# The second MoE's first product by Strassen's algorithm, its weight sums kept in DRAM

## Chip, cores and metric

The kernel runs on one core of a Trainium2 chip. The metric is the time of one execution on the device in microseconds, the median of several runs. A core has TensorE (PE, matmuls), VectorE (DVE), ScalarE (ACT), GpSimd (POOL) and the queues that issue DMAs, of which SyncE's (SP) is used most here.

## What is computed

Attention with rotary embedding, then two feed-forward layers. Only the last one is touched by the change:

```python
# q, k, v: (4, 8, 576, 64)
attn = softmax(rot(q) @ rot(k).T / 8) @ v
x = attn as (2304, 512)                       # 4 * 576 tokens, 8 * 64 features
# first MoE: w1, w2, w3 (512, 768), w_out (768, 512)
y = maximum(maximum(x @ w1, x @ w2), x @ w3) @ w_out
# second MoE: w_in (512, 2048), w_out (2048, 512)
h = y @ w_in
g = h / (1 + exp(-h))
out = g @ w_out                               # (2304, 512) float32
```

## The kernel before

The kernel works at more than float16 precision: each operand of a product is scaled by a power of two and split into a float16 high and low part (`split`, two instructions: the high part on ScalarE, the low part on VectorE), and a product is three float16 matmuls, high-high, high-low and low-high. A matmul here has a 128 x 128 stationary operand and a moving one of 256 or 320 columns.

The instructions are written in program order in a framework that places them on the engines with a planner of its own: an instruction that is ready by the planner's reckoning goes ahead of an earlier one that isn't, and each engine then runs its own list in the order fixed at build time. Buffers are rings with a fixed number of slots (`Ring`), and an instruction that takes a slot waits until the slot's last user is done. A PSUM bank is waited for as a whole.

Attention runs first, the first MoE (`moe1`) beside it, batch by batch, and its last batch alone. It computes `y` and stores it in the DRAM scratch `yscr`. Its groups go to five PSUM banks (rings `ps_m` and `ps_g`), and ScalarE (L548) and VectorE (L550, L557) evacuate them. In the attention part `narrow_w2` has turned the second MoE's weights into float32 and stored them in the DRAM scratches `zscr["wi"]` and `zscr["wo"]`.

Beside the last batch of `moe1` the weights of the second MoE are made ready. `load_w2` reads `w_in` back and splits its 16 pieces of 512 columns in place (`WI`, L154 and L159). `prep_wo7` makes the seven sums of four quarter blocks of `w_out` that Strassen's algorithm wants, in 8 tiles `w7[f]`: two loads, four differences of 256 columns (L758, on VectorE or GpSimd), two splits (L763, L764). Four of the tiles are made here, the other four beside the start of `moe2`.

`moe2` works in 9 blocks `jb` of 256 tokens, in four units `u` each. `s1(jb, u)` computes 4 of the 16 blocks of 128 features of `h`, each with 4 x 3 matmuls (L796), 48 in all, into two PSUM banks of one ring, and the next unit takes the other ring (`ps_m`, tag "m", and `ps_b`, tag "mb", two banks each). ScalarE applies Silu from PSUM (L797), GpSimd makes four sums (L803), ScalarE and VectorE split the seven forms in pieces of 768 and 1024 columns (L808, L809) into `g7`. `s2(jb, u)` computes the unit's share of the second product by Strassen's algorithm (Winograd's form): 7 products x 2 x 3 = 42 matmuls (L827), accumulated over the units in four banks `a`, `b`, `c`, `d`. `close(jb)` combines these (L836 to L846) and stores the block. In program order `s1` runs two units ahead of `s2`. `y_load` and `y_split` prepare `y` for 512 tokens at a time (largest magnitude over a block with L146 and `all_max`, which takes a slot of `ps_m`; four splits).

## Time and profile before

| | us |
|---|---|
| median of three runs | 1049.77 (1049.08 to 1051.04) |
| the profiled execution | 1053.66 |
| its span, first to last instruction | 1051.9 |
| TensorE busy in it | 983.7 |
| VectorE, ScalarE, GpSimd busy | 596.2, 585.1, 397.1 |
| mean granted TensorE clock | 0.972 |

The page gives the busy time of each engine over the whole span. A table of windows gives it for a chosen stretch, with the granted TensorE clock as a share of 2.4 GHz. The timeline lists instructions in order of time: start, duration, engine, line, tile written and tiles read, and in brackets how long the engine was idle before it and what released it. Groups of instructions give the mean duration of one form of one line.

### The profile page before, as it was taken

The page shows a single profiled execution, that of the slowest core. Times are in us where ns is not written, and L with a number is a line of the kernel's source. Part 1 is how long each engine was busy: PE and PEld are TensorE (multiplying, and loading weights), DVE is VectorE, ACT ScalarE, POOL GpSimd, SP SyncE. Part 2 cuts the span into 40 slices and gives each one's busy share as a digit, 9 for nine tenths or more (in the row PEclk, how much of TensorE's full clock was granted, in tenths as well). Part 3 has the DMA queues.
Part 4 walks back from the last instruction along what each step waited for, and adds up shares of the span by engine and source line. Part 5 has one row for each costly group of instructions (what it writes and reads, how often), then busy time and mean ns, then how long its engine had stood idle before and what let it go on. Part 6 is the DMA issues. An engine that isn't in the chain of part 4 may idle for free.

```text
span 1051.9 us, 18993 instructions
## 1 busy us (share of the span) xinstructions
PE 983.7 (94%) x7426; PEld 739.4 (70%) x7426; DVE 596.2 (57%) x1090; ACT 585.1 (56%) x1287; POOL 397.1 (38%) x420
## 2 busy tenths in 40 slices
...
GB/s 154 271 113 100 33 94 52 91 1 13 101 93 128 134 90 73 72 94 91 109 88 103 83 160 186 14 53 1 61 22 1 61 22 1 41 21 1 22 21 21
DMA packets 81129, 76.00 MB, mean 72 GB/s; under 512 B 44944, under 2 KB 62096, under 8 KB 80528
## 3 DMA queue, kind: packets, MB, share of 16 engines
...
q10 hardware_dynamic: 1504, 0.72, 0.2%
...
## 4 chain that ended last, share of the span: by engine, by line
PE 73%; DVE 6%; ACT 2%; DMA 2%; issue 2%; SPq 1%; POOL 0%; DVEq 0%; POOLq 0%; ACTq 0%
PE m L532 18%; PE mb L796 8%; PE m L796 8%; PE xp L463 6%; PE s L386 5%; PE a L827 4%; PE tr L444 4%; PE c L827 4%; PE b L827 4%; PE mg L532 3%; PE d L827 2%; PE xp L459 1%; PE s L383 1%; PE s L376 1%; DVE w L764 1%
## 5 line engine op out<-in xcount | busy, mean ns | idle before, releaser
L803 POOL TENSOR_TENSOR gs<-gs 128x256 f32<-128x256 f32 x144 | 131.1, 911 | 224.6 <-ACT gs L797 219.1
L532 PE MATMUL m<-x,w 128*128 128x256 f16 (+1 forms) x1380 | 196.2, 288 | 14.0 <-DVE t L550 6.1
L532 PEld LDWEIGHTS <-w 128*128 128x128 f16 x1632 | 158.9, 99 | 66.7 <-issue 26.1
L809 DVE SCALAR_TENSOR_TENSOR g<-gs,sg,g 128x768 f16<-128x768 f32 x72 | 97.8, 1361 | 172.9 <-ACT g L808 172.4
L796 PEld LDWEIGHTS <-wi 128*128 128x128 f16 x1656 | 161.9, 98 | 18.9
L827 PEld LDWEIGHTS <-g 128*128 128x128 f16 x1485 | 145.4, 98 | 20.9 <-DVE g L809 3.3
L208 POOL TENSOR_SCALAR z<-z 128x256 uint16<-128x256 uint16 x64 | 53.4, 835 | 249.5 <-DVE z L207 232.2
L396 DVE TENSOR_REDUCE nb<-s 128x2 f32<-128x1152 f32 (+1 forms) x80 | 98.8, 1235 | 63.3 <-PE s L386 44.3
L403 ACT ACTIVATE e<-s,nb 128x576 f32<-128x576 f32 x144 | 105.3, 737 | 34.3 <-DVE nb L396 24.0
L808 ACT ACTIVATE g<-gs,sg 128x768 f16<-128x768 f32 x72 | 74.9, 1041 | 72.1 <-POOL gs L803 71.0
L415 ACT ACTIVATE e<-e,rec 128x576 f32<-128x576 f32 x144 | 104.2, 767 | 18.0 <-DVE rec L413 17.8
L444 PE MATMUL tr<-ident,e 128*128 128x128 f32 x576 | 96.8, 289 | 14.0 <-ACT T L346 5.9
L444 PEld LDWEIGHTS tr<-ident,e 128*128 128x128 f32 x576 | 70.1, 147 | 47.0 <-issue 15.7
L796 PE MATMUL mb<-yt,wi 128*128 128x256 f16 x828 | 95.0, 273 | 0.0
L796 PE MATMUL m<-yt,wi 128*128 128x256 f16 x828 | 94.8, 273 | 0.0
L463 PE MATMUL xp<-pt,vd 128*64 128x256 f32 (+1 forms) x512 | 84.2, 425 | 0.0
L386 PE MATMUL s<-T 64*128 64x512 f32 x256 | 82.3, 687 | 0.0
L448 ACT ACTIVATE pt<-tr 128x384 f32<-128x384 f32 x119 | 56.1, 485 | 42.8 <-PE tr L444 42.3
L532 PE MATMUL m<-h,wo 128*128 128x256 f16 (+1 forms) x448 | 65.3, 286 | 0.1
L797 ACT ACTIVATE gs<-mb,ch 128x512 f32<-128x512 f32 x36 | 24.7, 686 | 70.6 <-PE mb L796 70.6
L532 PEld LDWEIGHTS <-wo 128*128 128x128 f16 x512 | 49.1, 98 | 20.1 <-issue 7.3
L463 PEld LDWEIGHTS xp<-pt,vd 128*64 128x64 f32 x512 | 36.9, 139 | 33.8 <-issue 16.3
...
## 6 DMA issues: line engine op xcount, KB each, us to landing
...
```

Source lines behind the costliest of these rows:

```text
L386: last["s"] = nc.tensor.matmul(s[:, o:o + 512], qs[r], kt[r], start=True, stop=True).ins
L396: x = nc.vector.tensor_reduce(out=nb[:, 0:m], in_=both(s, 0, 960, 576) if m > 1 else s[:, 0:576], op=ALU.max, axis=AX.X, negate=True)
L403: x = nc.scalar.activation(out=e[:, HK[g]], in_=s[:, SK[g]], func=AF.Exp, bias=nb[:, g:g + 1], accum_out=sm[:, g:g + 1])
L415: nc.scalar.activation(out=e[:, HK[g]], in_=e[:, HK[g]], func=AF.Copy, scale=r[:, g:g + 1])
L444: nc.tensor.transpose(tr[:, i * n:(i + 1) * n], e[0:n, c * P:(c + 1) * P], ident[0:n, 0:n])
L463: nc.tensor.matmul(xp[r, 0:n], v4[:, g, c, :], pt[:, c + 5 * g, :], start=False, stop=(c == 3))
L532: nc.tensor.matmul(ps[:, 0:n], l, r, start=(i == 0), stop=(i == len(passes) - 1))
L796: nc.tensor.matmul(ps[:, e * 256:e * 256 + 256], l, r, start=(i == 0), stop=(i == len(passes) - 1))
L803: nc.gpsimd.tensor_tensor(out=g[o], in0=g[x], in1=g[y], op=op)
L808: nc.scalar.activation(out=h, in_=x, func=AF.Copy, scale=sg)
L809: nc.vector.scalar_tensor_tensor(out=l, in0=x, scalar=sg, in1=h, op0=ALU.mult, op1=ALU.subtract)
L827: x = nc.tensor.matmul(ps, l, r, start=first, stop=last_, skip_group_check=True)
```

## The change

The ninth of the 256-token blocks stays as it was and is done first (`s1(u)`, block 0). The other eight form four blocks `J` of 512 tokens, A and B of 256 each, and their first product is done by Strassen's algorithm: the tokens in two halves, the 512 input features in two halves, the 2048 output features in two halves. Each of 8 steps `p` (`s1_pair`) computes one pair of 128-feature blocks for all 512 tokens: 7 products x 2 x 3 matmuls of 256 columns, into four banks, two of each of the rings "m" and "mb". ScalarE copies two results, VectorE adds six times and GpSimd once, and Silu runs from SBUF on `ga` and `gb`. `g_split` then does for each unit what `s1` did before: four GpSimd sums and the splits.

The weight side needs seven sums of four quarters of `w_in`. `prep_wi8` makes them in 8 tiles, each with four loads, four sums on GpSimd or VectorE and two splits of 1024 columns, and stores each tile (1 MB) in the DRAM scratch `w8scr`. `w8_load` reads a tile back for each step, 0.92 MB, into one of four slots; block 0 reads the four original quarters only. `prep_wo7` follows in the same chain, now all 8 tiles beside the last batch of `moe1`. The token side needs seven forms too: `y7_load`, `y7_sums` (largest magnitude, four GpSimd differences of 512 columns) and `y7_forms` (seven splits of 512 columns). The order of the units: steps p0 to p7 of A and B, with the second product of the previous B between p0, p1 and p2, and A's first unit after p3; then A's other three units.

```diff
+    w8scr = dram.tile([P, NF2 // 2, 2, 8, 256], F16, name="w8scr")
...
-    def load_w2(W, nm):
-        for i in range(0, W.m, 4):
-            nc.sync.dma_start(out=W.all[:, i * 512:(i + 4) * 512], in_=zscr[nm][:, i * 512:(i + 4) * 512])
-        for i in range(W.m):
-            split(W.h(i), W.l(i), W.t[i], W.s)
-            yield
...
+    def y_scales(r, w, st):
...
+        if w > 1:
+            sh = small.tile([P, 1], F32, tag="sh", name="sh")
+            nc.vector.tensor_scalar(out=sh, in0=s, scalar1=1.0 / w, scalar2=None, op0=ALU.mult)
+            s = sh
+        return s, sg, ch, co
+    SUMS = ((4, 0, 2, ALU.add), (6, 1, 0, ALU.subtract), (5, 4, 1, ALU.subtract), (7, 3, 5, ALU.subtract))
+    DIFFS = ((4, 0, 1), (5, 2, 4), (6, 2, 0), (7, 3, 5))
+    def halves(p):
+        return [(f // 4 * KC * 512, f % 4 * P) for f in (p, p + NF2 // 2)]
+    def prep_wi8(W, stage, out_p):
+        sw = const.tile([P, 1], F32, name="swi8")
+        nc.vector.tensor_scalar(out=sw, in0=W.s, scalar1=0.5, scalar2=None, op0=ALU.mult)
+        for p in range(NF2 // 2):
+            z = stage.tile([P, 8, 256], F32, tag="z7", name="z7")
+            for i, (o, n) in enumerate(halves(p)):
+                for a in range(2):
+                    nc.sync.dma_start(
+                        out=z[:, i + 2 * a].rearrange("p (c n) -> p c n", c=2),
+                        in_=zscr["wi"][:, o + a * DM * 2:o + (a + 1) * DM * 2].rearrange("p (c n) -> p c n", c=2)[:, :, n:n + P],
+                    )
+            yield
+            eng = nc.vector if p % 3 == 2 else nc.gpsimd
+            for o, x, y, op in SUMS:
+                eng.tensor_tensor(out=z[:, o], in0=z[:, x], in1=z[:, y], op=op)
+            yield
+            w = out_p.tile([P, 2, 8, 256], F16, tag="w8o", name="w8o")
+            for a, b in ((0, 4), (4, 8)):
+                h, l, x = flat(w[:, 0, a:b]), flat(w[:, 1, a:b]), flat(z[:, a:b])
+                nc.scalar.activation(out=h, in_=x, func=AF.Copy, scale=sw)
+                nc.vector.scalar_tensor_tensor(out=l, in0=x, scalar=sw, in1=h, op0=ALU.mult, op1=ALU.subtract)
+                yield
+            nc.sync.dma_start(out=w8scr[:, p], in_=w)
+            done8.append(p)
+    done8 = []
...
-            eng = nc.vector if f % 2 else nc.gpsimd
-            for o, x, y in ((4, 0, 1), (5, 2, 4), (6, 2, 0), (7, 3, 5)):
+            eng = nc.vector if f % 3 == 2 else nc.gpsimd
+            for o, x, y in DIFFS:
                 eng.tensor_tensor(out=z[:, o], in0=z[:, x], in1=z[:, y], op=ALU.subtract)
...
+        turn, w8 = [0], [w8_load(k) for k in range(4)]
+        total = HB * (1 + nb // 2)
+        def w8_next():
+            k = turn[0]
+            turn[0] += 1
+            return w8[k]
+        def w8_more():
+            if len(w8) < total and len(w8) < turn[0] + 4:
+                w8.append(w8_load(len(w8)))
+        def g_split(jb, u, g):
+            sm = sum_p.tile([P, 4, 256], F32, tag="gsum", name="gsum")
+            q = [g[:, i] for i in range(4)] + [sm[:, i] for i in range(4)]
+            for o, x, y, op in SUMS:
+                nc.gpsimd.tensor_tensor(out=q[o], in0=q[x], in1=q[y], op=op)
+            t = g7[jb, u] = g7_p.tile([P, 2, 7, 2, P], F16, tag="g7", name="g7")
+            for lo, hi, x in ((0, 3, flat(g[:, 1:4])), (3, 7, flat(sm))):
+                h, l = (t[:, i, lo:hi].rearrange("p a i n -> p (a i n)") for i in range(2))
+                nc.scalar.activation(out=h, in_=x, func=AF.Copy, scale=sg_t[jb])
+                nc.vector.scalar_tensor_tensor(out=l, in0=x, scalar=sg_t[jb], in1=h, op0=ALU.mult, op1=ALU.subtract)
+        def s1(u):
+            yt, _, ch, _ = st["y0"]
+            g = ga_p.tile([P, 4, 256], F32, tag="ga", name="ga")
+            ws = [w8_next() for _ in range(2)]
...
+            g_split(0, u, g)
+        def s1_pair(J, p):
+            forms, ch = sc[J]
+            u, e = divmod(p, 2)
+            A, B = 1 + 2 * J, 2 + 2 * J
+            if e == 0:
+                gA[J, u] = ga_p.tile([P, 4, 256], F32, tag="ga", name="ga")
+                if u % 2 == 0:
+                    gB[J, u // 2] = z_p.tile([P, 8, 256], F32, tag="z7", name="z7")
+            ga, gb = gA[J, u], gB[J, u // 2][:, u % 2 * 4:u % 2 * 4 + 4]
+            w = w8_next()
+            tags = dict(b=0, a=0, c=1, d=1)
+            ps = {}
+            for bank, place, a, b in PRODUCTS:
+                if bank not in ps:
+                    ring, tag = rings[tags[bank]]
+                    ps[bank] = ring.tile([P, 512], F32, tag=tag, name=tag)
+                o = ps[bank][:, place * 256:place * 256 + 256]
+                passes = []
+                for c in range(2):
+                    wh, wl = (w[:, x, a, c * P:c * P + P] for x in range(2))
+                    yh, yl = (forms[b][:, x, c] for x in range(2))
+                    passes += [(wh, yh), (wh, yl), (wl, yh)]
+                for i, (l, r) in enumerate(passes):
+                    nc.tensor.matmul(o, l, r, start=(i == 0), stop=(i == len(passes) - 1))
+            w8_more()
+            a, b, c, d = (ps[k].rearrange("p (a n) -> p a n", a=2) for k in "abcd")
+            tm = tm_p.tile([P, 4, 256], F32, tag="t1", name="t1")
+            place = lambda g, i: g[:, 2 * i:2 * i + 2, e * P:e * P + P]
+            two = lambda x: x.rearrange("p (t n) -> p t n", t=2)
+            add = lambda o, x, y: nc.vector.tensor_tensor(out=o, in0=x, in1=y, op=ALU.add)
+            nc.scalar.activation(out=tm[:, 0], in_=b[:, 0], func=AF.Copy)
+            add(tm[:, 1], a[:, 0], tm[:, 0])
+            add(place(ga, 1), two(a[:, 1]), two(tm[:, 0]))
+            add(tm[:, 0], b[:, 1], tm[:, 1])
+            nc.scalar.activation(out=tm[:, 2], in_=c[:, 0], func=AF.Copy)
+            add(place(ga, 0), two(c[:, 1]), two(tm[:, 0]))
+            add(tm[:, 3], tm[:, 1], tm[:, 2])
+            nc.gpsimd.tensor_tensor(out=place(gb, 0), in0=two(tm[:, 0]), in1=two(tm[:, 2]), op=ALU.add)
+            add(place(gb, 1), two(d[:, 0]), two(tm[:, 3]))
+            for g in (ga, gb):
+                x = g[:, :, e * P:e * P + P]
+                nc.scalar.activation(out=x, in_=x, func=AF.Silu, scale=ch)
+            if e:
+                g_split(A, u, gA.pop((J, u)))
+        def y7_load(J):
+            return y_load(1 + 2 * J, yr_p.tile([P, 8, 512], F32, tag="yr", name="yr"), 512)
+        def y7_sums(J, r):
+            s, sg, ch, co = y_scales(flat(r[:, 0:4]), 2, st)
+            for jb in (1 + 2 * J, 2 + 2 * J):
+                sg_t[jb], co_t[jb] = sg, co
+            for o, x, y in DIFFS:
+                nc.gpsimd.tensor_tensor(out=r[:, o], in0=r[:, x], in1=r[:, y], op=ALU.subtract)
+            return s, ch
+        def y7_forms(J, r, s, ch):
+            forms = {}
+            for _, _, _, b in PRODUCTS:
+                t = forms[b] = y7_p.tile([P, 2, 2, 256], F16, tag=f"y7{b}", name=f"y7{b}")
+                split(flat(t[:, 0]), flat(t[:, 1]), r[:, b + 1], s)
+            sc[J] = forms, ch
...
-        todo = [(jb, u) for jb in range(nb) for u in range(UNITS)]
-        SKEW = 2
-        for n in range(len(todo) + SKEW):
-            if n < len(todo):
-                jb, u = todo[n]
-                s1(jb, u)
-                for _ in range(3):
-                    next(wo_rest, None)
-                j, part = divmod(jb, 2)
-                if u == 0 and part == 0 and j + 1 < len(blocks):
-                    raws[j + 1] = y_load(j + 1, yr_p)
-                if u == 1 and part == 1 and j + 1 < len(blocks):
-                    yts[j + 1] = y_split(j + 1, raws.pop(j + 1), yt_p, st)
-            if n >= SKEW:
-                jb, u = todo[n - SKEW]
-                s2(jb, u)
-                if u == UNITS - 1:
-                    close(jb)
+        def second(jb, u):
+            if jb and jb % 2 == 0:
+                g_split(jb, u, gB[jb // 2 - 1, u // 2][:, u % 2 * 4:u % 2 * 4 + 4]) if (jb, u) not in g7 else None
+            s2(jb, u)
+            if u == UNITS - 1:
+                close(jb)
+        def rest_step(n):
+            for _ in range(n):
+                next(wo_rest, None)
+        raw = y7_load(0)
+        for n in range(UNITS):
+            s1(n)
+            rest_step(4)
+            if n == 1:
+                y7_forms(0, raw, *y7_sums(0, raw))
+            if n >= UNITS - 2:
+                second(0, n - UNITS + 2)
+        rest_step(99)
+        after = [(0, u) for u in range(2, UNITS)]
+        for J in range(nb // 2):
+            A, B = 1 + 2 * J, 2 + 2 * J
+            more = J + 1 < nb // 2
+            for p in range(HB):
+                s1_pair(J, p)
+                if p < 2:
+                    k = len(after) // (2 - p)
+                    for _ in range(k):
+                        second(*after.pop(0))
+                if p == 1 and more:
+                    raw = y7_load(J + 1)
+                if p == 3:
+                    second(A, 0)
+                if p == 5 and more:
+                    sums = y7_sums(J + 1, raw)
+            if more:
+                y7_forms(J + 1, raw, *sums)
+            for u in range(1, UNITS):
+                second(A, u)
+            after = [(B, u) for u in range(UNITS)]
+        for x in after:
+            second(*x)
...
-    w2_p = Ring(ctx, "w2_p", 1, side="right")
-    WI.place(w2_p)
-    yr_p, yt_p = Ring(ctx, "yr_p", 1, side="right"), Ring(ctx, "yt_p", 2, side="right")
-    w7, z7_p = {}, Ring(ctx, "z7_p", 2, side="right")
-    wi_prep = load_w2(WI, "wi")
-    wo_rest = prep_wo7(WO, Ring(ctx, "w7a", 1, side="right"), z7_p, w7, 0, 4)
+    right_p = lambda nm, bufs: Ring(ctx, nm, bufs, side="right")
+    z7_p, w7_p, yt_p, w8a = right_p("z7_p", 3), right_p("w7_p", 1), right_p("yt_p", 1), right_p("w8a", 2)
+    w8o_p = Ring(left, "w8o", 2)
+    w7, w8r = {}, [w8a, w8a]
+    def w8_load(k):
+        t = w8r[k % 4].tile([P, 2, 7, 256], F16, tag="w8s", name="w8s")
+        p = k % HB
+        if k < HB:
+            nc.sync.dma_start(out=t[:, :, 0:4], in_=w8scr[:, p, :, 0:4])
+        else:
+            nc.sync.dma_start(out=t, in_=w8scr[:, p, :, 1:8])
+        return t
+    preps = prep_wi8(WI, z7_p, w8o_p), prep_wo7(WO, w7_p, z7_p, w7, 0, HB)
+    chain = (x for p in preps for x in p)
+    early = {}
     n = 0
     for _ in moe:
         if n == 0:
-            y0 = y_load(0, yr_p)
-        next(wi_prep, None)
+            y0 = y_load(0, z7_p.tile([P, 8, 256], F32, tag="z7", name="z7")[:, 0:4].rearrange("p a n -> p (a n)").rearrange("p (a n) -> p a n", n=512), 256)
         n += 1
-        if n == 8:
-            st["y0"] = y_split(0, y0, yt_p, st)
-        if n > 16:
-            next(wo_rest, None)
-    for _ in wi_prep:
-        pass
-    for _ in wo_rest:
-        pass
+        if n == 4:
+            st["y0"] = y_split(y0, yt_p, st)
+        if n > 4:
+            for _ in range(1 + n % 2):
+                next(chain, None)
+    while len(done8) < HB:
+        next(chain)
+    for k in range(2):
+        early[k] = w8_load(k)
     left.close()
     tail.close()
-    wo_rest = prep_wo7(WO, Ring(ctx, "w7b", 1), z7_p, w7, 4, HB)
-    next(wo_rest)
+    w8b = Ring(ctx, "w8b", 2)
+    w8r += [w8b, w8b]
     ps_b, ps_a = Ring(ctx, "ps_b", 2, space=PSUM), Ring(ctx, "ps_a", 1, space=PSUM)
-    pools2 = (yr_p, yt_p) + tuple(Ring(ctx, nm, bufs) for nm, bufs in (("gs_p", 2), ("g7_p", 3), ("o_p", 2)))
-    moe2(st, pools2, ((ps_m, "m"), (ps_b, "mb")), ps_a, wo_rest, w7)
+    pools2 = (z7_p,) + tuple(
+        Ring(ctx, nm, bufs)
+        for nm, bufs in (("yr_p", 1), ("y7_p", 1), ("ga_p", 3), ("sum_p", 2), ("g7_p", 3), ("tm_p", 2), ("o_p", 1))
+    )
+    moe2(st, pools2, ((ps_m, "m"), (ps_b, "mb")), ps_a, chain, w7, lambda k: early.get(k) or w8_load(k))
```

## Rows read from the trace of the kernel before

**Rows 1.** The page: busy us of each engine, share of span, instructions.
```profile
PE 983.7 (94%) x7426; PEld 739.4 (70%) x7426; DVE 596.2 (57%) x1090; ACT 585.1 (56%) x1287; POOL 397.1 (38%) x420
```

**Rows 2.** Stretches by window: busy us of each engine, granted clock, DMA.
```profile
core 0: us, PE busy (x) PEld busy (x) DVE busy (x) ACT busy (x) POOL busy (x), PEclk, DMA share, GB/s
622.00:686.00 64.00, 63.31 (x506) 49.08 (x503) 45.20 (x85) 32.12 (x56) 9.68 (x10) 1.00 0.37 132
...
701.00:711.00 10.00, 6.94 (x52) 5.40 (x50) 10.00 (x8) 6.14 (x7) 7.75 (x7) 0.83 0.00 0
711.00:789.60 78.60, 78.60 (x721) 70.22 (x719) 33.68 (x41) 31.82 (x41) 32.30 (x35) 1.00 0.09 28
...
946.80:1025.40 78.60, 78.60 (x720) 70.22 (x719) 29.43 (x39) 30.70 (x40) 30.59 (x35) 1.00 0.06 15
```

**Rows 3.** Timeline of TensorE: start, duration, instructions merged. One unit at 711 us.
```profile
710.88 5.40 PE L796 MATMUL mb<-yt,wi 128*128 128x256 f16 x48
...
716.12 1.47 PE L827 MATMUL b<-w,g 128*128 128x256 f16 x12
...
720.70 0.38 PE L796 MATMUL m<-yt,wi2f 128*128 128x256 f16 x2
```

**Rows 4.** Timeline of TensorE around 706 us, in brackets the idle time before.
```profile
706.07 1.04 PE L827 MATMUL b<-w,g 128*128 128x256 f16 x4 [3.06 <-DVE g L809]
706.89 1.06 PE L827 MATMUL a<-w,g 128*128 128x256 f16 x4
```

**Rows 5.** Instruction groups by form, 712 to 1040 us: count, busy, mean ns, idle.
```profile
L803 POOL TENSOR_TENSOR gs<-gs 128x256 f32<-128x256 f32 x133 | 118.0, 887 | 183.2 <-ACT gs L797 178.0
...
L809 DVE SCALAR_TENSOR_TENSOR g<-gs,sg,g 128x768 f16<-128x768 f32 x33 | 46.9, 1421 | 126.7 <-ACT g L808 126.7
...
L809 DVE SCALAR_TENSOR_TENSOR g<-gs,sg,g 128x1024 f16<-128x1024 f32 x34 | 43.6, 1284 | 46.2 <-ACT g L808 45.7
...
L159 DVE SCALAR_TENSOR_TENSOR yt<-yr,ys,yt 128x512 f16<-128x512 f32 x12 | 9.9, 823 | 0.0
...
L146 DVE TENSOR_REDUCE ym<-yr 128x1 f32<-128x2048 f32 x2 | 4.6, 2286 | 4.4 <-DMA yr<-yscr 4.4
...
L839 DVE SCALAR_TENSOR_TENSOR tm<-b,co,ob 128x256 f32<-128x256 f32 x8 | 3.9, 484 | 0.1
```

**Rows 6.** Instruction groups by form, 622 to 700 us.
```profile
L159 DVE SCALAR_TENSOR_TENSOR wi<-wi,swis 128x512 f16<-128x512 f32 x15 | 12.3, 817 | 2.5 <-ACT wi L154 2.3
...
L764 DVE SCALAR_TENSOR_TENSOR w<-z,sw,w 128x1024 f16<-128x1024 f32 x7 | 8.9, 1276 | 12.9 <-ACT w L763 12.9
...
L758 DVE TENSOR_TENSOR z<-z 128x256 f32<-128x256 f32 x15 | 8.6, 598 | 3.8 <-DMA z<-zwo 3.8
...
L764 DVE SCALAR_TENSOR_TENSOR w<-z,sw,w 128x768 f16<-128x768 f32 x6 | 6.0, 1005 | 0.0
...
L550 DVE SCALAR_TENSOR_TENSOR t<-mg,t 128x256 f32<-128x256 f32 x4 | 1.6, 408 | 0.0
...
L548 ACT ACTIVATE t<-mg 128x256 f32<-128x256 f32 x3 | 1.0, 370 | 0.0
```

**Rows 7.** Timeline of all engines, 1030 to 1038 us: one unit's `g` chain.
```profile
1030.96 0.72 POOL L803 TENSOR_TENSOR gs<-gs 128x256 f32<-128x256 f32 x1 [4.28 <-ACT gs L797]
...
1032.61 1.47 PE L827 MATMUL b<-w,g 128*128 128x256 f16 x12
...
1032.81 0.69 ACT L797 ACTIVATE gs<-mb,ch 128x512 f32<-128x512 f32 x1 [1.93 <-PE mb L796]
...
1037.72 1.29 DVE L809 SCALAR_TENSOR_TENSOR g<-gs,sg,g 128x1024 f16<-128x1024 f32 x1 [1.80 <-ACT g L808]
```

**Rows 8.** DMA issues, 712 to 1040 us: count, KB each, median us to landing.
```profile
yr<-yscr SPq DMA_DIRECT2D x2, 1024.0 KB, 5.7
```

**Rows 9.** Timeline of TensorE, a wait in the first MoE.
```profile
312.02 1.76 PE L532 MATMUL m<-x,w 128*128 128x256 f16 x12 [4.10 <-DVE t L550]
```

77 lines of the change are left out of this document (32 added, 45 removed).

## The prediction

> **What bounds the kernel now.** I read the page first: TensorE is busy for 983.7 of the 1051.9 us span, VectorE for 596.2 [rows 1]. A share of the whole span says little, so I cut the trace into stretches. From 711 us on the second MoE runs, and there TensorE is busy for 78.60 of 78.60 us in every pass of 512 tokens (four equal windows, the first and the last stand in the rows), at a granted clock of 1.00 (the 2.4 GHz level), while VectorE and ScalarE are busy for 29 to 34 us and GpSimd for 31 to 32 [rows 2]. TensorE bounds this part, and nothing else comes near. The timeline gives the price: 48 matmuls from 710.88 to 716.12, then 42 until the next unit starts at 720.70, 90 in 9.82 us, 0.109 us each [rows 3]. A pass is 8 such units: 78.6 us, 720 matmuls.
>
> Two stretches ahead of this are not so clean. From 622 to 686 TensorE does the last batch of the first MoE (63.31 of 64 us busy), and VectorE, which evacuates for it, is already busy for 45.20 [rows 2]. From 701 to 711 TensorE is busy for 6.94 of 10 us: it waits 3.06 us for the first `g` piece (L809), and then runs four matmuls from 706.07 to 706.89, 0.205 us each, the 1.2 GHz level, with a granted clock of 0.83 over those 10 us [rows 2, 4]. VectorE is busy for all of the 10 us: the planner had put these matmuls where VectorE could not yet deliver.
>
> **What is removed.** In a block of 512 tokens the first product falls from 8 of 8 block products to 7 of 8: 7 x 2 x 3 = 42 matmuls for each of 8 steps `p`, 336, where two blocks had 2 x 192 = 384. The second product stays at 336. Four such blocks save 4 x 48 = 192 matmuls, the ninth block of 256 tokens saves none: 192 x 0.109 = 20.9 us. A pass becomes 672 matmuls, 73.3 us.
>
> **What is added to the other engines in a pass.** Each step has six VectorE adds of 256, most from PSUM; the nearest rows are 0.41 (L550) to 0.48 us (L839) [rows 5, 6]. 48 x 0.41 = 19.7 us, and 7 splits of 512 in place of 4 add 3 x 0.82 = 2.5. With 29 to 34 before, VectorE comes to 52 to 56 of 73.3 us. ScalarE gets 16 copies of 256 at 0.37 (L548) and 3 more splits, 8 us: 40 of 73.3; its Silu stays at 16 of 512 [rows 2, 6]. GpSimd gets 8 adds of 256 and 4 of 512: at 0.72 us alone or 0.89 on the mean [rows 5, 7] (and twice that for 512, an estimate) 11.5 to 14 us, in all 42 to 46. None reaches 73, so by sums TensorE stays the bound; what is lost is lost in waits.
>
> The weights come from DRAM in every step: 0.92 MB, four slots. A load is issued when its slot's step is done and is wanted three steps of 4.6 us later, 13.7 us at least; the nearest row lands 1 MB in 5.7 us [rows 8]. I cost it at nothing. On SP's queue it stands behind output stores that wait for `close`; the planner may turn that order badly, up to 2 us a pass.
>
> **Where the new waits are.** First, PSUM. Before, a unit alternated between two rings, and a bank had a whole unit of 9.8 us to be emptied. Now the four banks b, a, c, d are all used in every step, so bank b of the next step waits for this one. Of a step's 4.58 us, b is filled after 1.31, a after 2.62. A filled bank is picked up about 0.2 us after the next group begins (1032.61 to 1032.81 [rows 7]). Then three VectorE adds follow, the last of which reads b: 2.62 + 0.2 + 3 x 0.41 = 4.05, against 4.58. That leaves 0.5 us, less the way back to TensorE. If a split of 1.28 or 1.42 us (L809) is then on VectorE, b comes up to 1 us late. Only steps that follow directly on one another suffer, p2-p3 and p4 to p7, four boundaries a pass, 16 in all; elsewhere a second-product unit of 4.58 us lies between. The planner may also put matmuls of a later unit into the gap, as it mixes work elsewhere. Bounds 0 to 16; I take 0.3 each, 5 us.
>
> Second, the `g` chain. From Silu to the last split it takes 1032.81 to 1039.01, 6.2 us [rows 7]; the first unit of A has two steps, 9.2 us, of cover, the others more. Beside a busier VectorE each of four GpSimd sums may cost 0.2 us more, and the last split 0.4. Where the order was fixed without this, TensorE waits, as at 703. Bounds 0 to 3 us a pass; I take 0.5, 2 us. A wait as long as that at 703 lowers the clock too; 1 us for that in all. `y7_sums` holds one bank through its maximum, and its 2.29 us reduction stands on VectorE [rows 5]; it is ready early, so I leave it within these bounds.
>
> Third, the end of the first MoE. `prep_wi8` adds 16 VectorE splits of 1.28 and 8 sums of 0.60, 25 us, and takes away 16 of 0.82, 13; the other four `w7` tiles move forward from 687 us on, 4 x (1.28 + 1.00) = 9 us more; the half-sized first `y` takes 2.6 off [rows 6]. VectorE goes from 45 to about 64 of the 64 us between 622 and 686. The evacuations of the first MoE queue among these, with five PSUM banks to hide them; the nearest example of such a wait is 4.10 us at 312 [rows 9]. Bounds 0 to 6, I take 2. All eight tiles of `w8` have to pass VectorE and DRAM before the first block ends; the tail has the time for that.
>
> Fourth, the start. The four `w7` tiles leave the stretch 687 to 708, and the sums and seven splits of the first 512-token block come in: about 2.3 + 7 x 0.82 + 1 = 9 us on VectorE, what the tiles cost. So I leave the wait at 703 as it is; it may go (-4.7, with the slow clock) or double (+4.7).
>
> **The sum.** -20.9 + 5 + 2 + 1 + 2 = -10.9 us. The profiled execution took 1053.66 us, span 1051.9; it would become 1042.8. It lies 3.9 us above the median of the runs, 1049.77, so for the median I say 1038.9, rounded to 1039.
>
> **Rivals.**
> All of it is gained. The planner fills every gap, as in every pass before, and the lighter start loses its wait: -20.9, to -25.6 with the 4.7: 1024 to 1032. For it: after 711 no idle time at all. Against: the 16 tight boundaries.
>
> The gain is spent. The four kinds of waits reach 19 to 23 us, for instance 0.8 at each boundary, 1.5 a pass in the `g` chain: 1048 to 1052, no change. For it: TensorE's waits stand behind VectorE or ScalarE wherever VectorE is busy, 4.10 us being the longest [rows 9].
>
> Slower, by the single banks. If the split of `g` lies in the way at each of the 24 steps p2 to p7, 1.0 us late with the add pushed behind it, and nothing fills the gaps, that is 24 us, with 2 to 6 at the tail, up to 5 at the start and some slow clock: 1054 to 1066. It decides from 20.9 us, 0.65 per step over all 32. For it: the slack is half a microsecond and a split is over twice that. Against: half the steps have no neighbour.
>
> Slower, by VectorE and GpSimd in each other's way. The split of 768 elements takes 1.42 us where GpSimd's sums run beside it (L809) and 1.00 where few do (L764); a sum takes 0.72 alone and 0.89 on the mean; VectorE's 256 sums of two SBUF tiles 0.60 on the mean beside GpSimd [rows 5 to 7]. If the two took strict turns, a pass would need 16 splits (18 us), 8 adds (3.3), 7 splits (5.7) and 0.8 of such VectorE work, 28 us, after GpSimd's 36; alone that is 64 of 73 and fits. It turns the sign only if GpSimd also keeps VectorE from its other 24 us: 88 us a pass, 4 x (88 - 78.6) = +38, 1087. At the measured 0.42 us of delay for 33 such operations it is 14 us, VectorE at 66 of 73: not enough. The Trainium skill ("SBUF — State Buffer", section "SBUF: two separate sides") speaks here against the change: it calls the port pair that VectorE and GpSimd share an exclusive lock, held for the whole instruction, which a VectorE operation with two SBUF inputs has to take. By that rule the time would be this rival's. The trace agrees that they delay each other, by 0.42 us in 1.00, and so by less than a whole wait for a sum of 0.72.
>
> That the change doesn't save the matmuls is hardly possible: the count follows from the loops.
>
> **Chances.** Forecast (1033 to 1046) 0.51; all gained 0.13; spent 0.16, of which 0.05 still below 1047.7 and 0.10 within; slower by banks 0.16; slower by the two engines 0.04. Faster by over 0.2% (2.1 us, about what a measurement of this kernel can tell from no change) 0.69, within 0.10, slower 0.21. The range leaves out the lowest tail of "all gained" and the highest of the slower ones: 1028 to 1060.
>
> **What would show it.** Right: 192 fewer matmuls on TensorE; a pass of 73 to 77 us; TensorE idle before product b of steps p5 to p7, released by VectorE's adds, in pieces below 1 us; loads of `w8` that nobody waits for; VectorE at 70 to 80% in a pass. Wrong: a pass over 78 us; waits of TensorE for weights; idle time in the tail from 622 to 686 above 6 us; VectorE near 100% in a pass with its sums of two SBUF tiles far above 0.60. I am wrong downward if TensorE shows no idle time after the first block.

## The result, and the profile after

The changed kernel takes 1064.75 us (median of 4 runs, 1062.57 to 1068.4), the kernel before 1050.4 on the same chip: a ratio of 1.0126, interval 1.0095 to 1.0157. It is slower, by 14 us where 11 less were forecast. The profiled execution has a span of 1065.0 us. Its page, engines first, then the chain that ended last (to be set against [rows 1]):

```profile
PE 969.5 (91%) x7234; PEld 719.1 (68%) x7234; DVE 699.6 (66%) x1302; ACT 620.6 (58%) x1361; POOL 486.7 (46%) x500
...
PE 54%; POOL 11%; DVE 9%; ACT 4%; DMA 4%; issue 3%; SPq 1%; DVEq 0%; POOLq 0%; ACTq 0%
PE m L533 18%; POOL gsum L833 7%; PE xp L464 6%; PE m L886 5%; PE s L387 5%; PE tr L445 4%; PE mb L886 4%; PE a L942 2%; PE b L942 2%; PE c L942 2%; DMA z<-zwi 2%; POOL z L797 2%; DVE y L160 2%; DVE g L838 1%; PE xp L460 1%
```

The 192 matmuls are gone (7426 to 7234), and TensorE's idle time has grown by more than they took (68.2 to 95.5 us of the span). GpSimd's sums of `g` (L833) now stand on the chain with 7% of the span. The stretches, by window (engines' busy us and counts, granted clock, DMA share, GB/s):

```profile
622.00:686.00 64.00, 57.53 (x451) 44.39 (x449) 46.22 (x68) 31.46 (x45) 31.26 (x32) 0.97 0.81 255
738.59:1059.64 321.05, 307.93 (x2783) 270.20 (x2780) 213.08 (x358) 152.13 (x232) 171.77 (x183) 1.00 0.33 107
698.04:738.59 40.55, 34.37 (x280) 28.21 (x280) 34.54 (x41) 25.16 (x32) 33.97 (x29) 0.92 0.67 232
```

In the tail TensorE is busy for 57.53 of 64 us, where it was 63.31 [rows 2]; the load of DMA went from 0.37 to 0.81, GpSimd's from 9.7 to 31.3, and VectorE's stayed near 46 (45.20 before). In the four passes 13.1 us are idle, in the first block 6.2.

The attention of one and the same code ends between 611 and 620 us in different executions, so I compare lengths of stages and no absolute times. *Tail*: from the start of the attention's last group of `xp` products to the first matmul of the second MoE. *First block*: from there to the first Strassen step (the first matmul that reads forms of `y`). *Passes*: from there to the last matmul. Before: tail 620.02 to 685.92, 65.9; second MoE to 1046.53, 360.6. All stages of all kernels, us:

| kernel | median | tail | first block | passes | second MoE |
|---|---|---|---|---|---|
| before | 1050.4 | 65.9 | | | 360.6 |
| after | 1064.75 | 78.8 | 40.6 | 321.0 | 361.6 |
| e1 no preparation of `w_in` | 1050.32 | 76.0 | 31.2 | 322.2 | 353.4 |
| e2 no sums of `g` | 1053.10 | 77.3 | 37.9 | 315.0 | 352.9 |
| e3 four slots for sums | 1062.68 | 78.1 | 41.3 | 318.8 | 360.0 |
| e4 preparation last | 1065.13 | 76.7 | 36.3 | 329.1 | 365.4 |
| e5 turns | 1059.68 | 77.5 | 41.8 | 313.2 | 354.9 |
| e6 turns, other tail | 1058.00 | 76.6 | 31.8 | 327.7 | 359.5 |
| e7 no forms of `y` | 1053.66 | 77.6 | 41.9 | 311.7 | 353.6 |
| e8 `y` stores on ScalarE | 1062.27 | 76.8 | 37.2 | 327.6 | 364.9 |
| e9 `y0` late | 1062.73 | 82.4 | 34.7 | 321.3 | 356.0 |
| e10 preparation in attention | 1062.68 | 71.4 | 31.9 | 322.5 | 354.4 |
| e11 the same, turns | 1058.51 | 72.5 | 31.8 | 316.0 | 347.8 |
| e12 e10, no sums, no forms | 1044.86 | 71.3 | 32.3 | 303.1 | 335.4 |
| e13 no weights prepared | 1052.29 | 77.6 | 30.8 | 322.8 | 353.6 |
| e14 preparation, no sums | 1053.85 | 75.3 | 32.7 | 322.3 | 355.0 |
| e15 e11, early forms | 1058.63 | 71.2 | 31.7 | 317.8 | 349.5 |
| e16 e13, `y0` first | 1045.76 | 73.2 | 30.9 | 321.1 | 352.0 |
| e17 `y0` at group 8 | 1065.41 | 77.2 | 34.5 | 332.3 | 366.8 |

Where the first step comes early (e4, e6, e8, e17: 2811 to 2819 matmuls in "passes" against 2774 to 2783), 3 to 4 us of the first block are counted with the passes; there the last column is the one to read.

Each stage is read from one execution. The tail holds the same work in the changed kernel, e2, e3, e5 and e7 (77.3 to 78.8 us), and so do the passes in the changed kernel, e1, e9, e10, e13, e14 and e16 (321.0 to 322.8): between two kernels a difference of under 2 us in one stage shows nothing.

So the 14 us are: tail +12.9, second MoE +1.0. The second of these hides two large numbers. At 0.1091 us a matmul [rows 3], 3240 matmuls before take 353.5 and 3048 after 332.6: the 20.9 us are won, and what the second MoE takes beyond them has grown from 7.1 to 29.0 (TensorE's idle time alone from 3.1 to 19.3). What TensorE waited for, first in tail and first block, then in the passes (us in total, times, longest):

```profile
PE b L942 <- DVE g L838: 3.4, 3, 1.7
PE m L533 <- DVE ye L127: 3.2, 1, 3.2
PE mb L854 <- ACT y L575: 2.5, 1, 2.5
PE mg L533 <- DVE h L558: 2.5, 2, 1.6
PE mg L533 <- ACT h L557: 2.2, 2, 1.3
PE m L854 <- DMA w8s<-w8scr: 1.8, 1, 1.8
...
PE b L942 <- DVE g L838: 7.8, 10, 1.4
PE b L942 <- ACT g L837: 3.4, 3, 1.4
PE a L942 <- ACT g L837: 1.2, 1, 1.2
```

In the passes every wait is in a second product, for a split of `g`; no step (L886) waits for its banks. One of them, on TensorE, then VectorE, then GpSimd (start, duration, in brackets the idle time before):

```profile
803.30 0.38 PE L942 MATMUL b<-w,g 128*128 128x256 f16 x2
805.01 0.61 PE L942 MATMUL b<-w,g 128*128 128x256 f16 x4 [1.33 <-DVE g L838]
...
798.64 0.74 DVE L160 SCALAR_TENSOR_TENSOR y<-yr,sh,y 128x512 f16<-128x512 f32 x1
...
799.63 1.22 DVE L160 SCALAR_TENSOR_TENSOR y<-yr,sh,y 128x512 f16<-128x512 f32 x1
800.77 0.41 DVE L892 TENSOR_TENSOR ga<-mb,t 128x256 f32<-128x256 f32 x1
801.11 0.74 DVE L160 SCALAR_TENSOR_TENSOR y<-yr,sh,y 128x512 f16<-128x512 f32 x1
...
802.10 1.46 DVE L838 SCALAR_TENSOR_TENSOR g<-z,sg,g 128x768 f16<-128x768 f32 x1
803.48 1.48 DVE L838 SCALAR_TENSOR_TENSOR g<-ga,sg,g 128x768 f16<-128x768 f32 x1
...
802.02 2.12 POOL L833 TENSOR_TENSOR gsum<-ga 128x256 f32<-128x256 f32 x2 [1.72 <-ACT ga L904]
804.11 1.44 POOL L833 TENSOR_TENSOR gsum<-gsum,ga 128x256 f32<-128x256 f32 x1
```

The split that is wanted starts at 803.48. VectorE has no gap ahead of it: forms of the next `y`, adds of the step, another block's split. GpSimd sums at the same time, and 256 columns take it 1.06 and 1.44 us. Over the passes VectorE is busy for 213.1 of 321.1 us, two thirds; here it has no gap of over 0.1 us from 795 to 807, and is busy for 18.9 of the 20 us from 795.

Five of the 14 waits are of this kind, 5.9 of their 12.4 us. The other nine, 6.5 us, go back to GpSimd: its sums for several units run one behind the other, the splits on ScalarE and VectorE wait for them, and VectorE is busy for only 4 to 9 of the 10 us ahead of such a wait. One of them, four sums from the chain that ended last (start, duration) and the wait on TensorE:

```profile
825.86 4.40 POOL gsum L833 x4
...
828.42 0.39 PE L942 MATMUL b<-w,g 128*128 128x256 f16 x2 [1.15 <-ACT g L837]
```

In the 10 us ahead of it GpSimd is busy for 9.8, VectorE for 5.3 and ScalarE for 4.3.

### The profile page after: what moved, and what is told of

It is laid out like the page before. It is cut to its first block, busy times and chain, and to the rows that moved or that the text cites. A ratio compares the mean times of both kernels' runs of the same rounds, so it can differ in the third digit from the quotient of the medians.

```text
span 1065.0 us, 19287 instructions
## 1 busy us (share of the span) xinstructions
PE 969.5 (91%) x7234; PEld 719.1 (68%) x7234; DVE 699.6 (66%) x1302; ACT 620.6 (58%) x1361; POOL 486.7 (46%) x500
## 4 chain that ended last, share of the span: by engine, by line
PE 54%; POOL 11%; DVE 9%; ACT 4%; DMA 4%; issue 3%; SPq 1%; DVEq 0%; POOLq 0%; ACTq 0%
PE m L533 18%; POOL gsum L833 7%; PE xp L464 6%; PE m L886 5%; PE s L387 5%; PE tr L445 4%; PE mb L886 4%; PE a L942 2%; PE b L942 2%; PE c L942 2%; DMA z<-zwi 2%; POOL z L797 2%; DVE y L160 2%; DVE g L838 1%; PE xp L460 1%
## 5 line engine op out<-in xcount | busy, mean ns | idle before, releaser
L533 PE MATMUL m<-x,w 128*128 128x256 f16 (+1 forms) x1380 | 200.4, 291 | 17.2 <-DVE t L551 7.6
L209 POOL TENSOR_SCALAR z<-z 128x256 uint16<-128x256 uint16 x64 | 53.3, 833 | 251.5 <-DVE z L208 243.3
L886 PEld LDWEIGHTS <-w8s 128*128 128x128 f16 x1344 | 130.8, 98 | 17.1 <-issue 1.2
L397 DVE TENSOR_REDUCE nb<-s 128x2 f32<-128x1152 f32 (+1 forms) x80 | 98.8, 1235 | 65.2 <-PE s L387 46.4
L404 ACT ACTIVATE e<-s,nb 128x576 f32<-128x576 f32 x144 | 105.3, 737 | 34.7 <-DVE nb L397 25.0
L445 PEld LDWEIGHTS tr<-ident,e 128*128 128x128 f32 x576 | 69.6, 146 | 44.5 <-issue 13.1
L886 PE MATMUL m<-y,w8s 128*128 128x256 f16 x768 | 90.9, 273 | 0.4
L837 ACT ACTIVATE g<-gsum,sg 128x1024 f16<-128x1024 f32 x36 | 41.3, 1146 | 60.5 <-POOL gsum L833 60.5
L838 DVE SCALAR_TENSOR_TENSOR g<-gsum,sg,g 128x1024 f16<-128x1024 f32 x36 | 49.8, 1384 | 37.3 <-ACT g L837 37.1
L942 PE MATMUL b<-w,g 128*128 128x256 f16 x423 | 59.6, 274 | 15.7 <-DVE g L838 11.2
L886 PE MATMUL mb<-y,w8s 128*128 128x256 f16 x576 | 69.5, 273 | 0.2
L900 POOL TENSOR_TENSOR z<-t 128x256 f32<-128x256 f32 x32 | 27.8, 868 | 87.6 <-ACT t L897 53.2
L327 POOL TENSOR_TENSOR w<-qk,sin_sb 128x384 f32<-128x384 f32 (+1 forms) x44 | 45.2, 1048 | 33.9 <-DMA qk<-in_q_dram 27.9
```

Of the source, the lines that this page charges most:

```text
L397: x = nc.vector.tensor_reduce(out=nb[:, 0:m], in_=both(s, 0, 960, 576) if m > 1 else s[:, 0:576], op=ALU.max, axis=AX.X, negate=True)
L404: x = nc.scalar.activation(out=e[:, HK[g]], in_=s[:, SK[g]], func=AF.Exp, bias=nb[:, g:g + 1], accum_out=sm[:, g:g + 1])
L445: nc.tensor.transpose(tr[:, i * n:(i + 1) * n], e[0:n, c * P:(c + 1) * P], ident[0:n, 0:n])
L533: nc.tensor.matmul(ps[:, 0:n], l, r, start=(i == 0), stop=(i == len(passes) - 1))
L838: nc.vector.scalar_tensor_tensor(out=l, in0=x, scalar=sg_t[jb], in1=h, op0=ALU.mult, op1=ALU.subtract)
L886: nc.tensor.matmul(o, l, r, start=(i == 0), stop=(i == len(passes) - 1))
```

## Experiments

**What the preparation of the weights costs.** e1 leaves the preparation of `w_in` out and fills its scratch during the attention:

```
-    preps = prep_wi8(WI, z7_p, w8o_p), prep_wo7(WO, w7_p, z7_p, w7, 0, HB)
+    preps = (prep_wo7(WO, w7_p, z7_p, w7, 0, HB),)
```

> Leaves out the making of the weight sums: prep_wi8 is not called, and the DRAM scratch is filled during attention with finite float16 data from W1, so that the steps read as many bytes as before (the output is not the reference's). Everything behind the last batch of the first MoE stays as in the changed kernel. Theory A (about 12 us of the loss lie in that batch, made by prep_wi8): the second MoE's first matmul comes near 686 us in place of 698, and the time falls to 1049 to 1054 us. Rival (the eight w_out tiles or the planner's order do it, the weight sums do not): the first matmul stays behind 694, time 1060 to 1066.

Ratio 0.9985 (0.996 to 1.001): 14.4 us back in the median, by the stages 9.4 in the first block and 2.9 in the tail; the rest lies ahead of the tail, whose start differs between executions. The time is that of theory A, but the theory put the gain into the tail, and that stays at 76.0. The `w_out` tiles, now eight, are still made there: all three of its waits, 2.5, 2.3 and 3.3 us, end between 629 and 640, where readers of `y0`'s maximum and of the banks stand behind the splits of these tiles on VectorE and ScalarE.

e4 puts the whole preparation behind the last batch's groups (the `next(chain)` in the loop goes). e8 moves the last batch's `y` stores from SP's to ScalarE's queue:

```
-                nc.sync.dma_start(out=yscr[:, m, b * S + o:b * S + o + n], in_=ysb)
+                (nc.scalar if b == B - 1 else nc.sync).dma_start(out=yscr[:, m, b * S + o:b * S + o + n], in_=ysb)
```

> The chain of weight preparation stands behind the whole last batch in program order instead of between its groups, so the planner prefers the evacuations of the batch wherever both are ready. If the 12 us in this batch come from VectorE taking preparation first, the second MoE starts at 688 to 692 us and the time is 1054 to 1060 us, unless the later weights delay the first units. If they come from queues that stand behind late loads and sums whatever the preference, the time stays at 1062 to 1068 us or rises.

> One edit to the changed kernel: the last batch's stores of y go to ScalarE's DMA queue. If the 2.5 us wait ahead of the second MoE's first matmul is made by stores that stand behind the w_out loads on SyncE's queue, that wait goes: 1061 to 1063 us, first matmul at 695 us. Rival: the next waiter takes its place, 1064 to 1066.

e4: ratio 1.0146, tail 76.7, second MoE 365.4, with a wait of 5.0 us for a `w8s` load. e8: 1.0105 (1.0077 to 1.0133), tail 76.8. What e8 was after is in SP's queue of the changed kernel:

```profile
680.19 0.32 SPq L777 DMA_DIRECT2D w8scr<-w8o  x1
680.60 17.23 SPq L793 DMA_DIRECT2D z<-zwo  x8
697.87 0.90 SPq L576 DMA_DIRECT2D yscr<-y  x2
```

The stores stand behind loads that wait for a free tile, and with them the last `y`. On the other queue that wait falls from 2.5 to 0.5, the tail by 2.0, and waits for `w8s` in the first block, 4.6 us in place of 1.8, take it back.

The early wait, 3.2 us for `ye`, is a queue on VectorE:

```profile
629.11 1.79 DVE L775 SCALAR_TENSOR_TENSOR w8o<-z,swi,w8o 128x1024 f16<-128x1024 f32 x1 [1.57 <-ACT w8o L774]
630.82 0.27 DVE L116 TENSOR_REDUCE amax<-m 1x1 f32<-1x128 f32 x1
631.02 1.54 DVE L775 SCALAR_TENSOR_TENSOR w8o<-z,swi,w8o 128x1024 f16<-128x1024 f32 x1
634.36 1.35 DVE L775 SCALAR_TENSOR_TENSOR w8o<-z,swi,w8o 128x1024 f16<-128x1024 f32 x1 [1.80 <-ACT w8o L774]
635.63 0.14 DVE L127 TENSOR_SCALAR ye<-m 128x1 f32<-128x1 f32 x1
...
635.82 2.43 PE L533 MATMUL m<-x,w 128*128 128x256 f16 x12 [3.21 <-DVE ye L127]
```

The maximum of `y0` lies in one of the two `m` banks from 631 on; its reader stands behind two splits, one of which waits for ScalarE, and the first MoE wants the bank. The 12 matmuls behind the wait take 0.20 us each at a granted clock of 0.53, the 1.2 GHz level. e9 moves `y0` to groups 24 and 30, e17 its maximum to group 8, where it was before:

```
-        if n == 4:
+        if n == 8:
             st["y0"] = y_split(y0, yt_p, st)
```

> The first block's y is loaded and split about 26 groups later, behind the stretch in which the first sums for the weights are made; everything else is as in the changed kernel. If the maximum of y0, which holds one of the two general PSUM slots while VectorE stands in line, is what delays the tail, the two waits near 636 us (3.2 and 0.5) and the slow clock behind them go: tail 78.8 to about 73. If the tiles themselves (their sums, splits and transfers in the in-order queues) are the cause, the waits only move and the tail stays at 76 to 79.

> The changed kernel with the maximum of y0 at group 8 in place of 4, where the kernel before had it, and all preparation behind that. If y0's new place is what brings the wait near 636 (3.2, 0.5 and slow matmuls), it goes and the tail is 74 to 75. If the preparation of the weights in front of it on VectorE is, the wait comes at group 8 as well or is replaced by others, and the tail stays at 77 to 79.

The waits only move: tail 82.4 in e9 (for `ye` 2.0, `t` 2.2, `h` 3.3 us near the end) and 77.2 in e17, totals 1062.7 and 1065.4. e14 keeps loads, splits and stores of the preparation and leaves out its sums (the two loops `eng.tensor_tensor` over `SUMS` and `DIFFS`):

> The preparation of both weights without its sums (64 operations of 256 columns, two thirds on GpSimd, one third on VectorE): loads, splits and stores stay, and VectorE still has 32 splits. If the splits stand in the in-order queues behind the sums, and evacuations behind those, most goes: tail 68 to 70. If VectorE's splits and the transfers are too much for the tail whatever the order, it goes down by what VectorE saves, 5 to 6 tiles of 2.4 us at half weight: tail 73 to 76.

Tail 75.3: the second case, and 2 to 3.5 us is what the sums were worth. These waits stay, GpSimd doing nothing:

```profile
PE mb L848 <- ACT y L575: 3.4, 1, 3.4
PE m L533 <- DVE ye L127: 2.3, 1, 2.3
PE mg L533 <- ACT h L557: 1.6, 2, 1.4
PE mg L533 <- DVE h L558: 1.3, 2, 0.8
```

The total is 11 us better all the same: the first block falls from 40.6 to 32.7, as it no longer begins with a backlog. e13 prepares nothing and loads `w_out` tiles ready-made; e16 does so too, with `y0`'s maximum at group 8 and these loads behind it in program order. Of e13's edit:

```
             w = w7[f] = pool.tile([P, 2, 7, 256], F16, name=f"w7{f}")
-            for a, b in ((0, 4), (4, 7)):
...
+            nc.sync.dma_start(out=w, in_=w8scr[:, f, :, 0:7])
```

> No weight is prepared: the scratch of w_in is filled during the attention with other data by one DMA a tile, and the w_out tiles are loaded ready-made from it; all sums and splits of weights are gone, the loads stay. If the preparation is all that was lost ahead of the passes, the tail is 65 to 67 and the first block 30 to 32, and the total 1064.75 - 12.9 - 9 = 1043. If the first block's y in its new place or the weight loads cost something of their own, the tail stays above 69.

> As the run without any preparation of weights, but the maximum of y0 at group 8, as in the kernel before, and the ready-made w_out tiles loaded behind it, so that y0's load no longer stands behind them. If the preparation was all of the loss in the tail, it is 66 to 68 now (before 65.9), the first block 31, the passes as in the changed kernel (321 to 323), the total 1043. If y0's maximum costs by itself, a wait of 2 to 4 us for it stays, and the tail is 70.

The first block is as expected, 30.8 and 30.9. The tail isn't, and for one reason; VectorE in e13, and the DMAs issued from 605 to 640 us (KB each, us to landing):

```profile
631.08 1.22 DVE L147 TENSOR_REDUCE ym<-z 128x1 f32<-128x1024 f32 x1 [12.74 <-DMA z<-yscr]
...
w<-w8scr SPq DMA_DIRECT2D x8, 896.0 KB, 10.6
...
z<-yscr SPq DMA_DIRECT2D x1, 512.0 KB, 17.6
```

The eight loads share the DMA with `y0`'s, and the transposition for its maximum, next on TensorE, holds up everything behind it: 9.3 us. In e16 the wait is 5.0, as the maximum stands later in TensorE's list; the loads didn't change places. On SP's queue in e16:

```profile
608.64 5.35 SPq L793 DMA_DIRECT2D w<-w8scr  x8
614.12 0.54 SPq L714 DMA_DIRECT2D z<-yscr  x1
```

The tail of before, of e13, of e16 and of the changed kernel, as windows:

```profile
620.02:685.92 65.90, 65.21 (x519) 50.06 (x518) 45.45 (x86) 32.12 (x56) 11.55 (x12) 1.00 0.38 136
...
610.97:688.59 77.62, 67.19 (x516) 50.98 (x516) 18.40 (x44) 13.88 (x30) 0.00 (x0) 0.93 0.32 121
...
611.71:684.94 73.23, 67.10 (x516) 50.98 (x516) 18.32 (x44) 13.88 (x30) 0.00 (x0) 0.95 0.34 128
...
619.22:698.04 78.82, 67.41 (x518) 50.62 (x518) 57.33 (x82) 39.09 (x54) 40.93 (x39) 0.98 0.70 221
```

TensorE is idle for 0.7, 10.4, 6.1 and 11.4 us. The 6.1 of e16 are four waits around `y0`'s maximum (5.04, 0.37, 0.25, 0.47) and nothing else; the matmuls behind them, in part at the 1.2 GHz level (granted clock 0.66 on the mean from 634 to 641), are the 2 us more of TensorE's busy time. So without the preparation no other evacuation and no store is waited for. That the tail would be as long as before if `y0` came in time is a subtraction, 73.2 - 6.1 - 1.9 = 65.2, and not a run: no kernel with the new order had a tail below 71, and in each of them `y0` was waited for.

e10 makes the sums of `w_in` in half tiles during the attention, from about 470 us on, `w_out` four tiles in the tail and four in the first block, and `y0`'s maximum at group 8, as before:

```
+            for _ in range(2 if done8 else 0):
+                next(aprep, None)
...
-        if n > 4:
-            for _ in range(1 + n % 2):
-                next(chain, None)
+        if 16 < n <= 32:
+            next(chain, None)
```

> The weight sums are made in half tiles during the attention, from 470 us on, where VectorE is busy for about 60 percent; in the tail and the first block the w_out tiles are made as in the kernel before, four and four. The passes are as in the changed kernel. If the preparation alone is the cause of the loss ahead of the passes, the tail comes back to 66 to 68 and the first block to about 31 to 33, and the total is 1064.75 - 12 - 8 = 1045, with the passes still at 315 to 328. If something else of the change (the first block's own order, the transfer of the weights) is the cause, one of the two stays 5 us or more above that. If the attention has no room, its end moves by over 5 us.

Tail 71.4, first block 31.9: 16 us back. But the attention ends at 628.8 us, in all four kernels built this way at 628.8 to 630.3, where it was 611.0 to 620.0: 9 us or more of it go there. The total is 1062.68, where 1045 was expected. The preparation finds no free place, though in the kernel before VectorE is busy for only 22 to 30 of each 40 us from 380 to 580: TensorE is busy for 38 to 40 of them, and in e10 for 34.5 and 37.4 in two of the five.

And e10's tail is 5.5 us longer than before with less to prepare in it (VectorE busy for 42.8 us, before for 45.5). Five of its six waits end between 645 and 660; from 638 to 662, where the four `w_out` tiles are made, VectorE is busy for 21.5 of 24 us. This speaks for how close together the tiles stand, and not their number alone; no run spreads them out.

**What is lost in the passes.** e2 leaves out GpSimd's four sums of `g`, e7 the forms of `y` of the second to fourth block (the first block's stand in); e12 is e10 without both. e2's edit:

```
-            for o, x, y, op in SUMS:
-                nc.gpsimd.tensor_tensor(out=q[o], in0=q[x], in1=q[y], op=op)
...
-            for lo, hi, x in ((0, 3, flat(g[:, 1:4])), (3, 7, flat(sm))):
+            for lo, hi, x in ((0, 3, flat(g[:, 1:4])), (3, 7, flat(g))):
```

> Leaves out the four GpSimd sums of each g unit (the splits read the plain quarters again, so the output is not the reference's); number and size of the splits stay. Theory B (TensorE waits for g because GpSimd's sums come late): the four 512-token passes take 73 to 74 us each instead of about 78, 1043 to 1049 us in all. Rival (VectorE alone is late, by the adds of the steps and the splits): passes of 76 us or more, 1056 us or more.

> Leaves out the seven forms of y for the second to fourth block of 512 tokens (load, largest magnitude, four GpSimd differences, seven splits); the steps use those of the first block, so the output is not the reference's. If these 8 us of VectorE and 5 us of GpSimd per pass, placed where the units run side by side, are what makes the splits late, three passes get 4 us shorter each: 1050 to 1054 us. If the sums of g alone are late, less than 2 us each: 1059 to 1065.

> As the first kernel with the weight sums in the attention, and both GpSimd's four sums of g and the forms of y of the second to fourth block left out. If preparation, sums and forms are together all that was lost, the passes come to about 304 (302.4 is 2772 matmuls at 0.109) and the total to 1030. If the banks or the weight loads cost something of their own, the passes stay above 308.

e2: 1.0033 (1.0011 to 1.0054), passes 315.0; e7: 1.0037 (1.0018 to 1.0056), passes 311.7. Either gives back part, 6.0 and 9.3 of 18, and the waits that stay are the other's: in e2 steps that wait for ScalarE's and VectorE's forms of `y` (3.7) and for the step's adds into `ga` (3.6), in e7 second products that wait for a split of `g` (6.1). In e12 the passes take 303.1, and TensorE has no wait in them at all:

```profile
733.90:1037.00 303.10, 302.96 (x2774) 270.98 (x2771) 171.03 (x304) 136.34 (x210) 29.65 (x41) 1.00 0.32 101
```

So with these left out the banks, loads of the weights and the order of the steps cost nothing, and the sums and forms are all of the 18 us, where 6.0 and 9.3 together make 15.3. The total of 1044.86 (0.9947), where 1030 was expected, shows more: with perfect passes this change would win half a per cent, the rest being lost ahead of them.

Is it their place or their amount? e3 gives the sums four slots in place of two (a ring of three weight tiles pays for it). e5 puts one second-product unit behind every step and makes the splits two units ahead. e6 is e5 with the `y` stores as in e8 and the `w_out` tiles behind the batch. e11 is e10 with e5's order, e15 adds a second copy of four of the seven forms, made two or three steps earlier (with three weight tiles again). The core of e5:

```
+        def pump(t, last=False):
+            for x in queue[:3]:
+                if x[1] is None:
+                    jb, u = x[0]
+                    g_split(jb, u, raw_g.pop((jb, u)))
+                    x[1] = t
+            if queue and (last or queue[0][1] <= t - 2):
+                jb, u = queue.pop(0)[0]
+                s2(jb, u)
...
                 s1_pair(J, p)
+                pump(J * HB + p)
```

> Four slots in place of two for the sums of g; the room comes from the weight ring, three slots in place of four. Theory B1 (GpSimd has idle time in the steps, but its sums for the second half of a block can't be made early since a slot waits for its split): the waits in the second-product stretches fall by half or more, 1050 to 1058 us. Rival B2 (GpSimd and VectorE keep each other back whenever they run together, slots do not matter): within 3 us of 1064.75. Rival B3 (three weight slots are too few): TensorE waits for the weight loads, above 1068 us.

> Same work as the changed kernel, another order in the 512-token blocks: one unit of the second product after every step of the first, each unit's GpSimd sums and splits issued two units ahead of its use, in place of runs of three and four units side by side. Theory B (the four passes lose 18 us because the sums and splits of three or four units have to be made one after the other while TensorE already runs these units): the passes come to 74 to 76 us each, the time to 1049 to 1056 us; GpSimd stays below 13 of 20 us in every stretch. Rival (VectorE and GpSimd lose as much by running together, wherever the units stand): 1060 us or more.

> The order of e5, and two edits in the last batch of the first MoE: its stores of y go to ScalarE's DMA queue instead of SyncE's, where they stand behind loads that wait for a slot, and the w_out tiles come behind the batch in program order. If these two make the 3 to 7 us of waits seen from 681 to 698 us, the second MoE starts at 689 to 692 and the time is 3 to 7 us below e5. If the waits come from the weight sums alone, it is within 2 us of e5.

> As the run before, and one second-product unit behind every step in place of rows of three or four, with the splits of g two units ahead. If bunching is what costs in the passes, 8 us less than the run before: 1037, faster than the kernel before by 1.2 percent. If the planner only moves the waits elsewhere, the passes stay at 320 or above, and the total at 1045.

> As the run with the preparation in the attention and one second-product unit behind every step, and four of the seven forms of y have a second copy and are made at steps p4 and p5 of the pass before (paid for with a ring of three weight tiles in place of four). If the place of the forms is what costs, the passes fall from 316 to 308 and the total to 1050, the time of the kernel before; if their amount on VectorE costs, the passes stay at 314 to 318 and the total at 1057.

e3 (1.0122): GpSimd's sums fall from 7% to 1% of the chain and the passes by 2.2; the waits go over to the steps (for VectorE's adds 8.4 us, 6.0 of them for `ga`), and the second products wait for `g` for 1.3. e5 (1.008, 1.0051 to 1.011): passes 313.2, 7.8 less. e6 (1.01): second MoE 359.5, no gain of its own. e11 (1.0073, 1.0044 to 1.0101): passes 316.0, 6.5 below e10. e15 (1.008, 1.0051 to 1.0109): 317.8, nothing from the earlier forms. None of these beats the kernel before; e5, e6, e11 and e15 come nearest, at 1058 to 1060. The place is worth 6 to 8 of the 18 us.

Of the 10 us that e5's passes still take beyond e12's, 7.2 are five waits at two spots: four, 4.6 us, from 800 to 813, where VectorE is busy for 18.1 and GpSimd for 17.1 of 20 us, and one near the end, for the combine of the block before (`ob`):

```profile
812.24 0.39 PE L943 MATMUL b<-w,g 128*128 128x256 f16 x2 [1.95 <-ACT g L838]
...
1033.51 0.81 PE L943 MATMUL a<-w,g 128*128 128x256 f16 x6 [2.62 <-DVE ob L954]
```

Around 880 and 960, at the next two changes of block, e5 has no such wait. So what is left isn't lost in each pass, as it would be if the amount of the work alone cost it; the orders tried didn't remove these two spots, and why the first of the three changes of block has waits and the other two have none is open.

What the two engines do to each other is seen in the groups of the passes, first the changed kernel, then e12, where GpSimd is nearly idle (count, busy, mean ns):

```profile
L838 DVE SCALAR_TENSOR_TENSOR g<-ga,sg,g 128x768 f16<-128x768 f32 x17 | 22.3, 1313 | 12.5 <-ACT g L837 12.3
L892 DVE TENSOR_TENSOR t<-t 128x256 f32<-128x256 f32 x32 | 21.1, 660 | 0.0
L833 POOL TENSOR_TENSOR gsum<-gsum,ga 128x256 f32<-128x256 f32 x17 | 22.7, 1338 | 0.1
L900 POOL TENSOR_TENSOR z<-t 128x256 f32<-128x256 f32 x32 | 27.8, 868 | 87.6 <-ACT t L897 53.2 <-DVE t L892 34.4
```

```profile
L834 DVE SCALAR_TENSOR_TENSOR g<-ga,sg,g 128x768 f16<-128x768 f32 x16 | 16.3, 1018 | 26.2 <-ACT g L833 26.2
L888 DVE TENSOR_TENSOR t<-t 128x256 f32<-128x256 f32 x32 | 18.0, 562 | 0.7 <-ACT t L893 0.7
L896 POOL TENSOR_TENSOR z<-t 128x256 f32<-128x256 f32 x32 | 23.6, 738 | 203.5 <-DVE t L888 107.5 <-ACT t L893 95.9
```

A split of 768 takes 0.30 us longer beside the sums, an add of two SBUF tiles 0.10. GpSimd's add of a step goes from 0.74 to 0.87; its sums of `g` take 0.87 to 0.98 on the mean, one of the six forms 1.34.

## Why the prediction was wrong

*What is removed.* Right: 192 matmuls, 20.9 us, and 0.109 us each. In e12 the passes come to 303.1 for about 2774 matmuls.

*First, PSUM.* I took 5 us and bounds of 0 to 16; in the changed kernel it is nothing. The boundaries with 0.5 us of slack are filled with matmuls of the units before and after, which the sentence on the planner had allowed for; L886 is without a wait in the passes. Where the second products wait less, in e2 and e3, steps do wait for VectorE's adds as I had described, 4.2 and 8.4 us.

*Second, the `g` chain.* This is the first step that failed. I took 2 us, plus 1 for the clock, and 0 to 3 a pass; with the forms of `y` it cost about 18, 4.5 a pass. The chain of one unit was read from [rows 7], where it runs alone, and I gave it 9.2 us of cover. I had set VectorE's 56 and GpSimd's 46 us against a pass of 73 and concluded that what is lost is small. But a block of 512 tokens delivers its second half at once: four units of B with their sums, the seven forms of the next `y` and the adds of the steps fall into the stretch of second products, and there either VectorE has no gap (5.9 us of waits) or the splits wait for GpSimd, whose sums run one behind the other (6.5). The busy times I had right: VectorE 53.3, ScalarE 38.0 and GpSimd 42.9 us a pass, for which I had 52 to 56, 40 and 42 to 46. `y7_forms` I had counted as 5.7 us of VectorE's time and nowhere as a wait; by e7 leaving the forms out gives 9.3 us.

*Third, the tail.* The second that failed: 2 us, bounds 0 to 6; it was 12.9. My sum for VectorE itself, 64 of the 64 us to 686, was not reached (46.2, and 57.3 in the tail of 78.8; the rest slipped into the first block), and I put the excess at what five PSUM banks can hide. What I hadn't priced is the order of the queues: readers of `y0`'s maximum and of the banks behind splits that wait for ScalarE, stores behind loads that wait for a tile. In e16, without any preparation, all waits but those around `y0`'s maximum are gone, and the tail is 73.2; how much of the 12.9 is the preparation's and how much would stay with `y0` no run separates. By e14 the sums are 2 to 3.5 us of it. Moving the work within the tail or behind it (e4, e8, e9, e17) brings back about 2 us at most, or makes it worse.

*Fourth, the start.* I left the 4.7 us lost at 703 as they were, as the new work costs VectorE what the tiles had cost, with bounds of -4.7 to +4.7. The first block lost 9.7 (40.6 against the 30.9 of e16), 5.0 more than before. What I hadn't counted: it inherits the tail's backlog: VectorE is busy for 34.5 and GpSimd for 34.0 of its 40.6 us, and without the preparation of `w_in` (e1) the block takes 31.2.

*The weight loads.* Nothing, as I said, in the passes; in the first block 1.8 us.

Put together: -20.9 + 0 + 18 + 12.9 + 5.0 = +15.0; measured by the stages +13.9, by the medians +14.3. The last 1.1 I can't place: in its second MoE the kernel before has a single wait, the 3.06 us at 706.

*The signs.* Two of those named for being wrong came: passes of 80 us on the mean, and 6.5 us of idle time from 622 to 686. Waits for weights came only in the first block, and VectorE is at 66% of the passes.

*The rivals.* The one on the single banks had about the right time (1054 to 1066) by luck: its mechanism, TensorE waiting for the banks, didn't occur. The one on strict turns of VectorE and GpSimd (1087) didn't come: in the passes against e12 the splits of 768 lose 0.30 us (17 times) and 0.23 (16 times, 1.25 against 1.02), those of 1024 0.09 (34 times) and the adds 0.10 (32 times): 15 us over four passes, 4 a pass, where I had 14 from a delay of 0.42. The lock of the Trainium skill ("SBUF — State Buffer", section "SBUF: two separate sides") is so borne out in its direction: operations of two SBUF inputs get longer, and those that read PSUM keep 0.42; a whole wait for each sum isn't seen here on the mean.

I would have been right to ask for each stretch of 20 us, and not for a pass, what VectorE and GpSimd have to do there.
